# Weights decoded and split by a new plan, and earlier FFN units, in a thresholded attention with FFN

## The chip, the cores and the metric

The kernel runs on one core of a Trainium2 chip. The metric is device time in microseconds (us) from start to end of one execution. TensorE (PE) multiplies, VectorE (DVE), ScalarE (ACT) and GpSimd (POOL) work elementwise, SyncE (SP) issues the DMAs.

## What is computed

```python
def _attn_ref(q, k, v, tau):                 # 8 batches, 8 heads, 576 rows, 64 columns
    scores = scale * np.matmul(q, k.transpose(0, 1, 3, 2))
    thresh = np.max(scores, axis=-1, keepdims=True) - tau
    scores = np.where(scores >= thresh, scores, -1000000000.0)
    attn = np.exp(scores - np.max(scores, axis=-1, keepdims=True))
    attn = attn / (np.sum(attn, axis=-1, keepdims=True) + 1e-09)
    return np.matmul(attn, v)

def _moe_ref(x, w_in, w_out):                # 4608 tokens; w_in 512 x 2048, w_out 2048 x 512
    h = x @ w_in
    g = h * (1.0 / (1.0 + np.exp(-h)))
    return g @ w_out
```

The heads' results, put side by side, are the tokens x of the second function. The weights arrive as 64-bit floats, and the products are kept near fp32 by splitting operands into an upper and a lower f16 part.

## The kernel before

**Attention.** Work goes by tiles of 128 score rows of a head. A tile goes through: scores (L452 or L464, into one of two PSUM slots), row maximum (`soft1`, L474), exponential (L484, ScalarE), threshold and row sum (`soft2`, L493, VectorE, which frees the PSUM slot), normalising (`soft2b`), transposing (`soft3`), and, once a pair of heads is through, the product with v (`av`) and its split into x (`av_post`, L568 and L569). Batch 0 takes a "direct" form: its probabilities stay fp32, GpSimd normalises them (L507), TensorE transposes them (L403, L408) and ScalarE copies them out of PSUM (L416, L417). From batch 1 on ScalarE normalises (L511), GpSimd splits (L519 to L525) and DMAs transpose.

Batch 0 is worked in two halves: tiles 0 to 15 ("low") give x for its first 256 tokens, tiles 28 to 47 ("high") for the other 320. The indices 16 to 27 and 48 carry no tile; batch 1 begins at tile 49. The last index is about 300.

**Weights.** There are 16 chunks of w_in and 16 of w_out, 512 KB each. `load_weights` brings a chunk into a buffer: eight of w_in's into parts of `gbuf`, which later holds the FFN's inner values, the others in turn into two buffers of the pool `stage`. `decode_weights` turns 64-bit words into fp32: ScalarE L190, VectorE L193 and L196, then four matmuls (L208) whose diagonals give maxima. After 16 chunks `pow2_scales` makes a power-of-two scale of them (i_w for w_in, o_w for w_out). `split_weights` then makes the f16 parts in `wst`: for w_in GpSimd scales (L225), ScalarE rounds (L228), GpSimd subtracts (L229); for w_out ScalarE rounds with the scale (L220) and VectorE scales and subtracts in one instruction (L221).

**FFN.** A unit `h_unit` is 12 matmuls (L593) for 128 inner columns of one token range, with four elementwise steps behind it (L601 ScalarE, L602 VectorE, L608 ScalarE, L609 VectorE); a unit `o_unit` is 12 matmuls (L624), a quarter of the work for 128 output rows. For each of batch 0's two ranges there are 16 of each.

**What sets the order.** The main loop goes through the tile indices and writes, at each, the steps of a few tiles, the weights' steps that `W_PLAN` puts there, and as many FFN units as `credit` allows: it grows by `rate` per index, for batch 0 by `RATES`. A row of `W_PLAN` is first chunk, index of the first decode, index of the last, index at which the split ends, and a priority. A scheduler with a simulated timeline then orders each engine's instructions by these priorities and by what it holds to be ready; each engine runs its own list in that order. SP issues all loads in its list's order.

```python
W_PLAN = ((0, 0, 10, 13, 0), (16, 9, 22, 36, 0))
PRI_S, PRI_SOFT1, PRI_SOFT2 = 1600, 50, 200
```

## Time and profile before

| | |
|---|---|
| median of 3 runs | 1228.44 us (1227.75 to 1228.84) |
| the profiled execution: time | 1225.66 us |
| its span, first to last instruction | 1223.9 us |
| busy: PE, DVE, ACT, POOL | 1150.3, 933.7, 796.4, 707.5 us |
| mean granted TensorE clock, share of full | 0.987 |

Times of single instructions come from the profiled execution. The granted clock is the one of TensorE's two levels (1.2 and 2.4 GHz), as a share of the full one, averaged over a stretch. An engine's busy time in a stretch, set beside the stretch's length, tells whether it could have set the pace there; what ended the idle time ahead of an instruction tells whom it waited for.

### The profile page before, as it was taken

How to read it: one execution, taken by the hardware profiler on the slowest of the kernel's cores; microseconds unless marked ns; L12 is line 12 of the kernel's file. 1: busy time of each engine (PE TensorE's matmuls, PEld its weight loads, DVE VectorE, ACT ScalarE, POOL GpSimd, SP SyncE). 2: the span in 40 equal slices, each digit the busy share in tenths (PEclk: the TensorE clock that was granted, in tenths of full speed). 3: DMA queues.
4: the chain of work that ended last, by engine and by line, in shares of the span. 5: the costliest groups of instructions: out<-in, count | busy, mean ns of one | idle time of the engine just before them, and what ended most of it. 6: DMA issues, size and time to landing. Idle time of an engine off the chain costs nothing.

```text
span 1223.9 us, 27062 instructions
## 1 busy us (share of the span) xinstructions
PE 1150.3 (94%) x9474; PEld 899.2 (73%) x9474; DVE 933.7 (76%) x2625; ACT 796.4 (65%) x1505; POOL 707.5 (58%) x902
## 2 busy tenths in 40 slices
PE   6868799999899799999999999999999999999998
PEld 4545567777786577787777777788778877777777
DVE  7988988988999988889889858886788858333330
ACT  6667875876867777777777747785677756333331
POOL 2385357887877587886888428781778547100000
PEclk9979999999999999999999999999999999999999
DMA  9553148889788777886987448772877356200000
GB/s 309 185 161 95 41 108 173 160 160 177 132 177 141 160 137 139 150 165 151 167 149 145 114 94 155 146 136 82 153 150 142 77 92 116 42 11 16 16 10 25
DMA packets 340887, 151.73 MB, mean 124 GB/s; under 512 B 305936, under 2 KB 317200, under 8 KB 340752
## 3 DMA queue, kind: packets, MB, share of 16 engines
q1 hardware_dynamic: 340752, 150.01, 59.1%
q8 instruction: 75, 1.23, 0.4%
q14 instruction: 60, 0.49, 0.1%
HBM read 66.19 MB, written 9.44 MB: 62 GB/s over the span
## 4 chain that ended last, share of the span: by engine, by line
PE 63%; DVE 11%; DMA 10%; POOL 7%; issue 4%; ACT 4%; SPq 1%; POOLq 0%; ACTq 0%; DVEq 0%
PE o L624 24%; PE h L593 21%; PE s L464 9%; PE a L550 7%; DMA wT<-hl 4%; POOL hl L522 3%; DMA wraw<-in_w_out 3%; DVE w L493 2%; POOL hl L519 2%; DVE sm L474 2%; DVE qstack L350 2%; POOL hl L525 1%; DMA wraw<-in_w_in 1%; ACT w L484 1%; ACT w L511 1%
## 5 line engine op out<-in xcount | busy, mean ns | idle before, releaser
L593 PE MATMUL h<-x,wst 128*128 128x288 f16 (+2 forms) x3072 | 425.8, 288 | 7.8 <-DVE gbuf L609 5.0
L624 PE MATMUL o<-gbuf,wst 128*128 128x288 f16 (+2 forms) x3072 | 417.9, 286 | 2.4 <-ACT wst L634 2.4
L593 PEld LDWEIGHTS <-wst 128*128 128x128 f16 x3072 | 292.2, 98 | 95.7 <-issue 16.9
L624 PEld LDWEIGHTS <-wst 128*128 128x128 f16 x3072 | 292.7, 98 | 83.7 <-issue 7.4
L522 POOL TENSOR_TENSOR hl<-w,hl 128x512 f16<-128x512 f32 x252 | 302.6, 1201 | 12.8
L519 POOL TENSOR_SCALAR hl<-w 128x576 f16<-128x576 f32 x252 | 172.2, 686 | 193.4 <-ACT w L511 115.7
L484 ACT ACTIVATE w<-s,sm 128x576 f32<-128x576 f32 x288 | 211.6, 739 | 91.9 <-DVE sm L474 39.1
L493 DVE SCALAR_TENSOR_TENSOR w<-s,sm,w 128x576 f32<-128x576 f32 x288 | 232.0, 812 | 39.9 <-ACT w L484 37.8
L474 DVE TENSOR_REDUCE sm<-s 128x1 f32<-128x576 f32 x288 | 214.4, 749 | 28.7 <-PE s L464 21.8
L511 ACT ACTIVATE w<-w,sm 128x576 f32<-128x576 f32 x252 | 191.4, 771 | 52.1 <-DVE sm L501 50.1
L602 DVE SCALAR_TENSOR_TENSOR h<-th,h 128x288 f32<-128x288 f32 (+2 forms) x256 | 116.2, 455 | 113.7 <-ACT th L601 112.3
L601 ACT ACTIVATE th<-h,msc 128x288 f32<-128x288 f32 (+2 forms) x256 | 126.6, 498 | 103.2 <-PE h L593 101.8
L464 PE MATMUL s<-khi,qstack 128*128 128x288 f32 x560 | 144.3, 338 | 12.7 <-DVE w L493 9.9
L608 ACT ACTIVATE gbuf<-h 128x288 f16<-128x288 f32 (+2 forms) x256 | 104.3, 408 | 78.2 <-DVE h L602 77.5
L609 DVE SCALAR_TENSOR_TENSOR gbuf<-h,gbuf 128x288 f16<-128x288 f32 (+2 forms) x256 | 115.3, 452 | 41.9 <-ACT gbuf L608 41.0
L550 PE MATMUL a<-wT,v 128*64 128x288 f16 (+2 forms) x1568 | 115.0, 289 | 10.8 <-DMA wT<-hl 10.6
L360 POOL TENSOR_TENSOR klo<-kraw,khi 128x576 fp32r<-128x576 f32 x64 | 94.5, 1476 | 47.1 <-ACT khi L358 47.0
L464 PE MATMUL s<-klo,qstack 128*128 128x288 f32 x560 | 120.8, 296 | 0.0
L464 PEld LDWEIGHTS s<-khi,qstack 128*128 128x128 f32 x560 | 87.7, 190 | 31.9 <-issue 15.4
L550 PEld LDWEIGHTS <-v 128*64 128x64 f16 x1568 | 84.5, 110 | 33.7 <-issue 22.1
L464 PEld LDWEIGHTS s<-klo,qstack 128*128 128x128 f32 x560 | 90.4, 189 | 0.6
L525 POOL TENSOR_TENSOR hl<-w,hl 128x64 f16<-128x64 f32 x252 | 89.5, 355 | 0.0
(101 smaller groups left out, 930.4 us busy)
## 6 DMA issues: line engine op xcount, KB each, us to landing
kraw<-in_kT SPq DMA_DIRECT2D x128, 144.0 KB, 3.0
qraw<-in_qT SPq DMA_DIRECT2D x96, 144.0 KB, 3.0
vraw<-in_vL SPq DMA_DIRECT2D x32, 320.0 KB, 3.6
wraw<-in_w_out SPq DMA_DIRECT2D x16, 512.0 KB, 3.7
out_t<-wst SPq DMA_DIRECT2D x48, 144.0 KB, 2.1
wT<-hl SPq DMA_TRANSPOSE x280, 3.4
gbuf<-in_w_in SPq DMA_DIRECT2D x8, 512.0 KB, 6.2
wraw<-in_w_in SPq DMA_DIRECT2D x8, 512.0 KB, 5.1
```

The costliest lines, as they stand in the source:

```text
L464: nc.tensor.matmul(s_ps[:, j, :HALF], lhs, kk[:, j * HALF : (j + 1) * HALF], start=(n == 0), stop=(n == len(seq) - 1),)
L474: nc.vector.tensor_reduce(out=negm, in_=s_ps[:, :, :HALF], op=ALU.max, axis=AX.XY, negate=True)
L484: nc.scalar.activation(wtile[t].rearrange("p (j c) -> p j c", j=2), sps[t][:, :, :HALF], AF.Exp, bias=small[t][:, 0:1],)
L493: nc.vector.scalar_tensor_tensor(out=w3, in0=s_ps[:, :, :HALF], scalar=sm[:, 1:2], in1=w3, op0=ALU.is_ge, op1=ALU.mult, accum_out=sm[:, 2:3],)
L511: nc.scalar.activation(w, w, AF.Copy, scale=r)
L519: nc.gpsimd.tensor_scalar(out=fl[:, 0:S], in0=w, scalar1=1.0, scalar2=1.0, op0=ALU.mult, op1=ALU.mult)
L522: nc.gpsimd.tensor_tensor(out=fl[:, 640:1152], in0=w[:, 0:512], in1=fl[:, 0:512], op=ALU.subtract)
L550: nc.tensor.matmul(a_ps[odd * D : (odd + 1) * D, :n], vt[:, lo_v, odd, kv, :], wT[v, b * H + 2 * p + odd][:, kw, c0 - base : c0 - base + n ...
L593: nc.tensor.matmul(ph[:, :n], wi(c, f, lo_w), x16[b, lo_x][:, c, c0 : c0 + n], start=(k == 0), stop=(k == 11),)
L601: nc.scalar.activation(th[:, :n], ph[:, :n], AF.Tanh, scale=moe_sc[b][:, 0:1])
L602: nc.vector.scalar_tensor_tensor(out=ph[:, :n], in0=th[:, :n], scalar=1.0, in1=ph[:, :n], op0=ALU.add, op1=ALU.mult,)
L624: nc.tensor.matmul(ps[:, :n], wo(f, d, lo_w), g[:, lo_g, :n], start=(f == 0 and k == 0), stop=(f == NF - 1 and k == 2),)
```

## The change

- `RATES` goes from 0.9 units per index to 1.03 for the first range of batch 0 and to 1.45 for the second; and the first matmul of each of these units is held in program order against the others (`PACED`).
- The second row of `W_PLAN` gives w_out's loads, decodes and scale a priority of 150, and its split ends at index 38 instead of 36; the split itself has priority 0.
- Of the weights' chunks, those with i % 4 of 2 and 3 that had no place in `gbuf` get one (words 6400 and 7424), beside the two buffers of `stage`.
- The scale of w_out takes its column sum in the second half of the bank of the last weights' maximum instead of a bank of its own.
- `split_weights`: every second chunk of w_in goes the way that w_out went (ScalarE with the scale, L224, VectorE in one instruction, L225). The other eight stay with GpSimd (L230, L236). A chunk of w_out is now scaled by VectorE in fp32 (L234), rounded by ScalarE (L235), and subtracted by GpSimd (L236).
- `soft2b`: tiles 12 to 15 and 28 to 37 are normalised by ScalarE (L518) instead of GpSimd (L514, formerly L507).
- The direct tiles' transposes are written one index later, their product with v one later, and the FFN units that need it one later.

```diff
-RATES = (0.9, 0.9)
+PACED = 1
+RATES = (1.03, 1.45)
...
-W_PLAN = ((0, 0, 10, 13, 0), (16, 9, 22, 36, 0))
+W_PLAN = ((0, 0, 10, 13, 0), (16, 9, 22, 38, 150))
...
-        allp = bank([P, P], f"{name}_ps", own)
+        allp = wps[7][:, P : 2 * P] if name == "o_w" else bank([P, P], f"{name}_ps", own)
...
+        else:
+            o = (None, None, 6400, 7424)[i % 4]
+        if o is not None:
             t = gbuf.bitcast(I32)[:, o : o + 1024].rearrange("p (c w) -> p c w", w=2)
...
-        if i >= 4 * NK:
+        if i < 4 * NK and i % 2:
             nc.scalar.activation(hi, w, AF.Copy, scale=sc)
             nc.vector.scalar_tensor_tensor(
                 out=w16[:, i, 512:1024], in0=w, scalar=sc, in1=hi, op0=ALU.mult, op1=ALU.subtract
             )
             return
-        nc.gpsimd.tensor_scalar(
-            out=w, in0=w, scalar1=sc, scalar2=1.0, op0=ALU.mult, op1=ALU.mult
-        )
+        if i < 4 * NK:
+            nc.gpsimd.tensor_scalar(
+                out=w, in0=w, scalar1=sc, scalar2=1.0, op0=ALU.mult, op1=ALU.mult
+            )
+        else:
+            nc.vector.tensor_scalar(out=w, in0=w, scalar1=sc, scalar2=None, op0=ALU.mult)
         nc.scalar.activation(hi, w, AF.Copy)
         nc.gpsimd.tensor_tensor(
             out=w16[:, i, 512:1024], in0=w, in1=hi, op=ALU.subtract
...
-        if tiles[t][0] in direct:
+        if tiles[t][0] in direct and not 12 <= t < first_high + 10:
...
+                if b < PACED and k == 0:
+                    tc.keep_in_program_order(mm)
...
-            avs.setdefault(last_b + AV_LAG, []).append((v, p, c0, n))
+            avs.setdefault(last_b + AV_LAG + 1, []).append((v, p, c0, n))
             if p == NPAIR - 1:
-                ready.append((last_b + AV_LAG + 1, b, c0, n))
+                ready.append((last_b + AV_LAG + 2, b, c0, n))
...
-            at(t1 + i * (t2 - t1) // 16, pri(hp, lambda i=i + first: split_weights(i)))
+            at(t1 + i * (t2 - t1) // 16, pri(0, lambda i=i + first: split_weights(i)))
...
-        if live(t - 1):
+        if live(t - 1) and tiles[t - 1][0] not in direct:
             soft3(t - 1)
+        if live(t - 2) and tiles[t - 2][0] in direct:
+            soft3(t - 2)
```

How the engines' lists change is shown at three places. In the names, `w32_14` is the probability tile of tile 14, `sm` its row statistics, `wst` the weights, `s_33` the scores of tile 33, `th` and `h` an h unit's values (batch, first token, unit), `tm` and `tl` the transposed tile, `wT` its place in SBUF, and `o_0_0_1` the second 128 output rows of the first range.

GpSimd, from the normalising of the last low tiles on, before:

```order
L507 TENSOR_SCALAR w32_12_708<-w32_12_708,sm_12_707 128x576
L507 TENSOR_SCALAR w32_13_754<-w32_13_754,sm_13_753 128x576
L225 TENSOR_SCALAR wst_89<-wst_89,i_w_sc_612 128x512 x16
L229 TENSOR_TENSOR wst_89<-wst_89 128x512 x2
L507 TENSOR_SCALAR w32_14_795<-w32_14_795,sm_14_794 128x576
L507 TENSOR_SCALAR w32_15_839<-w32_15_839,sm_15_838 128x576
L507 TENSOR_SCALAR w32_28_1137<-w32_28_1137,sm_28_1136 128x576
L507 TENSOR_SCALAR w32_29_1154<-w32_29_1154,sm_29_1153 128x576
```

and after:

```order
L514 TENSOR_SCALAR w32_10_558<-w32_10_558,sm_10_557 128x576
L514 TENSOR_SCALAR w32_11_628<-w32_11_628,sm_11_627 128x576
L230 TENSOR_SCALAR wst_89<-wst_89,i_w_sc_597 128x512 x8
L236 TENSOR_TENSOR wst_89<-wst_89 128x512 x20
L514 TENSOR_SCALAR w32_38_1554<-w32_38_1554,sm_38_1553 128x576
L236 TENSOR_TENSOR wst_89<-wst_89 128x512 x4
L514 TENSOR_SCALAR w32_39_1591<-w32_39_1591,sm_39_1590 128x576
L514 TENSOR_SCALAR w32_40_1628<-w32_40_1628,sm_40_1627 128x576
```

The 16 scalings of w_in have become eight, the subtractions of w_in and w_out stand together in one piece of 20, and the normalisings of tiles 12 to 37 are gone from the list.

VectorE, around the threshold steps (L493, now L500) of tiles 32 and 33, before:

```order
L193 TENSOR_SCALAR wst_89<-wst_89 128x512
L213 TENSOR_REDUCE wmx_90<-wps_6_857 128x1
L196 SCALAR_TENSOR_TENSOR wst_89<-wraw_28_886,wst_89 128x512
L493 SCALAR_TENSOR_TENSOR w32_32_1287,sm_32_1286<-s_32_1244,sm_32_1286,w32_32_1287 128x576
L609 SCALAR_TENSOR_TENSOR gbuf_61<-h_0_0_0_944,gbuf_61 128x256
L497 TENSOR_SCALAR sm_32_1286<-sm_32_1286 128x1
L501 RECIPROCAL sm_32_1286<-sm_32_1286 128x1
L493 SCALAR_TENSOR_TENSOR w32_33_1328,sm_33_1327<-s_33_1290,sm_33_1327,w32_33_1328 128x576
L474 TENSOR_REDUCE sm_34_1372<-s_34_1331 128x1
```

and after:

```order
L576 SCALAR_TENSOR_TENSOR x16_0_1_472<-a_0_3_0_904,xscale_98,x16_0_0_471 128x256
L484 TENSOR_SCALAR sm_33_1322<-sm_33_1322,ntau_81 128x1
L309 SCALAR_TENSOR_TENSOR msc_0_762<-msc_0_762,o_w_sc_981 128x1
L234 TENSOR_SCALAR wst_89<-wst_89,o_w_sc_981 128x512 x14
L225 SCALAR_TENSOR_TENSOR wst_89<-wst_89,i_w_sc_597 128x512
L234 TENSOR_SCALAR wst_89<-wst_89,o_w_sc_981 128x512
L611 SCALAR_TENSOR_TENSOR h_0_0_0_924<-th_0_0_0_958,h_0_0_0_924 128x256
L611 SCALAR_TENSOR_TENSOR h_0_0_1_945<-th_0_0_1_1000,h_0_0_1_945 128x256
L234 TENSOR_SCALAR wst_89<-wst_89,o_w_sc_981 128x512
L500 SCALAR_TENSOR_TENSOR w32_32_1278,sm_32_1277<-s_32_1237,sm_32_1277,w32_32_1278 128x576
L500 SCALAR_TENSOR_TENSOR w32_33_1323,sm_33_1322<-s_33_1281,sm_33_1322,w32_33_1323 128x576
```

The last decodes no longer stand here; 16 scalings of w_out (L234) and a subtraction of w_in (L225) stand ahead of tile 32's threshold step. The 16 steps of w_out's split on VectorE before (L221) stood one or two at a time between the steps of tiles 39 to 47.

ScalarE, from the exponential of tile 44 on, before:

```order
L484 ACTIVATE w32_44_1772<-s_44_1742,sm_44_1771 128x576
L220 ACTIVATE wst_89<-wst_89,o_w_sc_1002 128x512
L416 ACTIVATE wT_6_5_1680<-tm_42_1747 128x4x128
L417 ACTIVATE wT_6_5_1680<-tl_41_1716 128x128
L484 ACTIVATE w32_45_1815<-s_45_1775,sm_45_1814 128x576
L220 ACTIVATE wst_89<-wst_89,o_w_sc_1002 128x512
L608 ACTIVATE gbuf_61<-h_0_0_8_1178 128x256
L601 ACTIVATE th_0_0_9_1278<-h_0_0_9_1219,msc_0_788 128x256
L416 ACTIVATE wT_7_6_1787<-tm_43_1780 128x4x128
L417 ACTIVATE wT_6_5_1680<-tl_42_1752 128x128
L608 ACTIVATE gbuf_61<-h_0_0_9_1219 128x256
L417 ACTIVATE wT_7_6_1787<-tl_43_1785 128x128
```

and after:

```order
L491 ACTIVATE w32_44_1782<-s_44_1752,sm_44_1781 128x576
L424 ACTIVATE wT_6_4_1643<-tl_40_1724 128x64
L424 ACTIVATE wT_6_5_1728<-tl_40_1724 128x64
L423 ACTIVATE wT_6_5_1728<-tm_41_1757 128x4x128
L617 ACTIVATE gbuf_61<-h_0_0_14_1393 128x256
L610 ACTIVATE th_0_0_15_1493<-h_0_0_15_1436,msc_0_762 128x256
L491 ACTIVATE w32_45_1827<-s_45_1785,sm_45_1826 128x576
L424 ACTIVATE wT_6_5_1728<-tl_41_1762 128x128
L423 ACTIVATE wT_6_5_1728<-tm_42_1790 128x4x128
L617 ACTIVATE gbuf_61<-h_0_0_15_1436 128x256
L645 ACTIVATE wst_89<-o_0_0_0_1480,msc_0_762 128x256
L645 ACTIVATE wst_89<-o_0_0_1_1646,msc_0_762 128x256
```

Where ScalarE was at the ninth and tenth h unit and still rounding w_out, it now does the last two h units and the first two outputs. Counted on TensorE's list: ahead of tile 40's scores stand 84 h matmuls instead of 36, ahead of tile 49's 192 h and 120 o matmuls instead of 144 and none.

## Rows read from the trace of the kernel before

**Rows 1.** Busy time, share of span and instructions of each engine (page)

```profile
PE 1150.3 (94%) x9474; PEld 899.2 (73%) x9474; DVE 933.7 (76%) x2625; ACT 796.4 (65%) x1505; POOL 707.5 (58%) x902
```

**Rows 2.** By stage: length; busy PE, PEld, DVE, ACT, POOL; PEclk, DMA share, GB/s

```profile
0.00:61.30 61.30, 46.10 (x285) 30.45 (x285) 51.54 (x166) 38.58 (x75) 16.59 (x30) 0.97 0.76 247
61.30:118.00 56.70, 42.42 (x233) 26.66 (x233) 46.90 (x117) 38.82 (x80) 43.23 (x44) 0.85 0.42 132
118.00:157.00 39.00, 31.56 (x213) 23.91 (x212) 34.87 (x92) 30.63 (x69) 9.98 (x9) 0.96 0.17 48
157.00:325.90 168.90, 157.04 (x1298) 122.86 (x1297) 148.59 (x421) 125.34 (x236) 132.68 (x164) 0.99 0.79 157
325.90:495.00 169.10, 156.96 (x1340) 122.97 (x1337) 153.61 (x429) 121.67 (x221) 125.90 (x163) 0.99 0.76 147
495.00:1223.90 728.90, 716.22 (x6116) 572.37 (x6115) 498.16 (x1404) 441.39 (x828) 379.16 (x494) 1.00 0.54 104
```

**Rows 3.** Timeline of TensorE: start, length, operation, idle before and releaser

```profile
61.28 1.24 PE L452 MATMUL s<-kd,gbuf 128*128 128x288 f32 x4 [0.85 <-DVE w L493]
...
118.05 1.24 PE L452 MATMUL s<-kd,gbuf 128*128 128x288 f32 x4
...
157.01 0.51 PE L464 MATMUL s<-khi,qstack 128*128 128x288 f32 x2
...
178.62 1.27 PE L624 MATMUL o<-gbuf,wst 128*128 128x256 f16 x10
```

**Rows 4.** Groups of ScalarE, 61.3 to 118 us: busy, mean ns, idle before

```profile
L190 ACT ACTIVATE wst<-wraw 128x512 f32<-128x512 f32 x14 | 9.4, 675 | 11.3 <-DMA wraw<-in_w_out 11.3
```

**Rows 5.** The chain that ended last, 52 to 113 us: start, length, what

```profile
52.62 3.47 DMA wraw<-in_w_out
...
56.59 4.51 DMA wraw<-in_w_out
...
112.50 1.31 PE h L593 x12
```

**Rows 6.** Timeline of GpSimd

```profile
60.02 12.72 POOL L225 TENSOR_SCALAR wst<-wst,i_w_sc 128x512 f32<-128x512 f32 x16 [2.51 <-DVE i_w_sc L145]
...
75.39 3.67 POOL L507 TENSOR_SCALAR w<-w,sm 128x576 f32<-128x576 f32 x4
```

**Rows 7.** Groups of VectorE, 0 to 61.3 us

```profile
L193 DVE TENSOR_SCALAR wst<-wst 128x512 int32<-128x512 int32 x18 | 7.9, 436 | 1.2 <-ACT wst L190 1.1
L196 DVE SCALAR_TENSOR_TENSOR wst<-wraw,wst 128x512 int32<-128x512 int32 x10 | 7.0, 698 | 0.0
```

**Rows 8.** Groups of VectorE, 61.3 to 118 us

```profile
L196 DVE SCALAR_TENSOR_TENSOR wst<-wraw,wst 128x512 int32<-128x512 int32 x14 | 13.2, 946 | 0.1
L193 DVE TENSOR_SCALAR wst<-wst 128x512 int32<-128x512 int32 x14 | 10.0, 712 | 6.3 <-ACT wst L190 6.3
...
L602 DVE SCALAR_TENSOR_TENSOR h<-th,h 128x256 f32<-128x256 f32 x3 | 1.2, 421 | 0.0
```

**Rows 9.** The weights' tile on VectorE, 0 to 160 us: duration ns min/median/max

```profile
L193 DVE TENSOR_SCALAR wst<-wst x32: 404/426/1281, 11.8 to 108.1; 128x512 int32<-128x512 int32 x32
L196 DVE SCALAR_TENSOR_TENSOR wst<-wraw,wst x24: 666/690/1527, 21.7 to 109.2; 128x512 int32<-128x512 int32 x24
L221 DVE SCALAR_TENSOR_TENSOR wst<-wst,o_w_sc x16: 726/743/1485, 124.6 to 150.3; 128x512 f16<-128x512 f32 x16
```

**Rows 10.** Groups of ScalarE, 0 to 200 us

```profile
L228 ACT ACTIVATE wst<-wst 128x512 f16<-128x512 f32 x16 | 10.0, 634 | 1.9 <-POOL wst L229 1.9
...
L601 ACT ACTIVATE th<-h,msc 128x256 f32<-128x256 f32 x16 | 7.3, 469 | 2.9 <-PE h L593 2.7
L511 ACT ACTIVATE w<-w,sm 128x576 f32<-128x576 f32 x9 | 6.8, 768 | 4.1 <-DVE sm L501 4.1
```

**Rows 11.** Groups of GpSimd, 61.3 to 118 us

```profile
L229 POOL TENSOR_TENSOR wst<-wst 128x512 f16<-128x512 f32 x16 | 21.4, 1355 | 3.6 <-ACT wst L228 3.6
...
L507 POOL TENSOR_SCALAR w<-w,sm 128x576 f32<-128x576 f32 x13 | 10.6, 822 | 8.2 <-DVE sm L501 3.3 <-DVE sm L497 2.7 <-PE tl L408 1.2
```

More of the change, by code (lines that the diff above doesn't have):

```diff
@@ L203, in decode_weights @@
         if c == 0:
-            wps[n] = bank([P, P], f"wps_{n}", 2)
+            wps[n] = bank([P, 2 * P if n == 7 else P], f"wps_{n}", 2)
         upper = w.bitcast(BF16).rearrange("p (c t) -> p c t", t=2)[:, :, 1]
@@ L208, in decode_weights @@
             nc.tensor.matmul(
-                wps[n], part, part,
+                wps[n][:, 0:P], part, part,
                 start=(c == 0 and j == 0), stop=(c == 3 and j == 3),
@@ L212, in decode_weights @@
         if c == 3:
-            nc.vector.tensor_reduce(out=wmx[:, n : n + 1], in_=wps[n], op=ALU.max, axis=AX.X)
+            nc.vector.tensor_reduce(out=wmx[:, n : n + 1], in_=wps[n][:, 0:P], op=ALU.max, axis=AX.X)
     def split_weights(i):
@@ L592, in h_unit @@
             for lo_w, lo_x in ((0, 0), (0, 1), (1, 0)):
-                nc.tensor.matmul(
+                mm = nc.tensor.matmul(
                     ph[:, :n], wi(c, f, lo_w), x16[b, lo_x][:, c, c0 : c0 + n],
@@ L623, in o_unit @@
             for k, (lo_w, lo_g) in enumerate(((0, 0), (0, 1), (1, 0))):
-                nc.tensor.matmul(
+                mm = nc.tensor.matmul(
                     ps[:, :n], wo(f, d, lo_w), g[:, lo_g, :n],
@@ L627, in o_unit @@
                 )
+                if b < PACED and f == 4 * quarter and k == 0:
+                    tc.keep_in_program_order(mm)
         def post():
```

## The prediction

> **What bounds the kernel now.** I read the busy shares first, then the stages, then the waits. TensorE is busy 94% of the span [rows 1], so only time that TensorE loses can be won. Where it loses it stands in the stage table [rows 2]. From 495 us on it is busy 716 of 728.9 us: little is to be had there. The first 157 us lose most: 46.10 busy of 61.3, 42.42 of 56.7, 31.56 of 39.0, thus 36.9 us idle, and part of the busy time ran at the lower of the two clock levels (mean granted clock 0.97, 0.85 and 0.96; of the busy time that is 3, 15 and 4%, or 1.4 + 6.4 + 1.3 us). The stages from 157 to 495 lose 24 us of 338.
>
> The borders of the stages are landmarks of the program on TensorE: the scores of tile 28 (first of the second half of batch 0) at 61.28, of tile 40 at 118.05, of tile 49 (first of batch 1) at 157.01; the first output unit of the FFN starts at 178.62 [rows 3]. The work in the two middle stages is not long; it is late. Three reasons can be read. ScalarE's decodes wait 11.3 us for the DMAs of w_out [rows 4]: with two buffers a load starts only after the decode of the one before last, and the chain of waits is made of such loads, 3.5 to 4.5 us each [rows 5]. GpSimd then scales 16 chunks of w_in in one go, 12.72 us from 60.02 on, with the normalising of tiles 14, 15, 28 and 29 queued behind it until 75.39 [rows 6]. And VectorE pays for sharing with GpSimd: a decode pair (L193, L196) costs 0.436 + 0.698 us in the first stage and 0.712 + 0.946 in the second, where GpSimd is busy 43.2 of 56.7 us [rows 2, 7, 8].
>
> **The change, part by part.** (1) Start to tile 28. The order now puts 28 decode pairs ahead of VectorE's step on tile 14, which frees the banks that tile 28 needs, instead of 18. This part costs: ten L193 at 0.436 and eight to nine L196 at 0.698 are 10 us [rows 7]; 2 us of that fit where VectorE is idle (51.54 busy of 61.3 [rows 2]). Tile 28 starts at 69 instead of 61.3. If VectorE's gaps took 4 us it would be 67; at the shared prices of [rows 8], 0.712 + 0.946, it would be 74, for there is a second cause for delay: the DMA engines are already 76% busy in this stage [rows 2] and the extra loads come on top.
>
> (2) Tile 28 to 40. VectorE is the longest here: 46.9 of 56.7 us [rows 2]. What goes: the decodes done earlier, ten L193 and eight L196 at the shared prices, 7.1 + 7.6 = 14.7 us [rows 8]. What comes: all 16 scalings of w_out in fp32 (L234), a form that the trace does not show. Its bounds are the single-input L193 of the same tile width, 404 ns at the least and 1281 at the most [rows 9]; I take 0.7, the mean of L193 beside a busy GpSimd [rows 8]: 11.2 us. Eight subtractions of w_in that leave GpSimd, at 743 ns, L221's median [rows 9]: 5.9 us. Four more h units with two steps of 0.42 each [rows 8]: 3.4 us. Sum 46.9 - 14.7 + 20.5 = 52.7 us. ScalarE, 38.8 us: ten decodes leave, 0.675 each [rows 4]; 12 normalisings at 0.768 (9.2), some 13 copies of w_out's upper parts at L228's 0.634 (8.2) and four h units with two steps of at most 0.47 (3.8) come [rows 10]: 53.2. GpSimd, 43.2 us: 13 normalisings, eight scalings and eight subtractions leave, 10.7 + 6.4 + 10.8; 16 subtractions at 1.355 come: 37 [rows 2, 6, 11], 20 subtractions stand in one piece. So VectorE and ScalarE fill the stage. Of VectorE's 9.8 us of idle time 6.3 were waits for a decode on ScalarE [rows 8], which itself waited for loads [rows 4]; with the loads ahead these go, and 52.7 + 3.5 = 56.2 us are left. With L234 at L193's median of 0.43 the stage takes 52, with 1.2 it takes 64. I take 57: tile 40 at 126 instead of 118. What hides the normalisings on ScalarE is the idle time that the loads leave; if the loads still come late, their 9.2 us fall on the chain to the transposes.
>
> (3) Tile 40 to 49. Here the faster rates of units tell. By the order, TensorE has 192 h matmuls and 120 o matmuls ahead of tile 49's scores, where it had 144 and none: 168 more, of which 48 lie ahead of tile 40. Twelve take 1.31 us [rows 5], so one takes 0.109 and the 120 of this stage 13.1 us; nine transposes fall behind, about 1 us less. TensorE's 31.56 us [rows 2] become 43.7, less the 1.3 that the low clock took: 42.4, and at 0.98 busy, as from 495 on, 43.3. VectorE's 34.87 [rows 2] lose the 16 L221, 11.9 us at their median [rows 9], and cannot hold this up. The stage is bound by TensorE: 43.5 us, between 41.5 and 46. Tile 49 starts at 169.5 instead of 157.0.
>
> (4) After tile 49. By then TensorE has done 168 x 0.109 = 18.3 us more FFN work, less 0.8 of transposes that stand behind: 17.5. So the end moves by 169.5 - 157.0 - 17.5 = -5.0 us if the rest takes what it took. By the order the lead stays at some 18 us of TensorE work to tile 140, is 11 at tile 150 and nothing by tile 216, so most of it is consumed after 495 us, where TensorE is 98% busy and less work is less time. I take the rest as neutral, by +-4.
>
> (5) At no cost: the maximum in half of a bank (same instructions), the four added buffer slots (no instruction), and the two delays of one tile for the transposes and the attention product. What hides these is that TensorE has h units to do meanwhile; without that cover, one tile of 4.3 us (39.0 / 9) once.
>
> The profiled execution took 1225.66 us, its span is 1223.9, and the median of the runs is 1228.44; the difference of 2.8 us lies between runs, so I move the median: 1228.4 - 5 = 1223.4, rounded to **1223**. By the bounds of the parts (67 to 74, 52 to 64, 41.5 to 46) the sum alone could run from -14 to +9.5 us.
>
> **Rivals.** *Dense fill, much faster.* If the earlier loads and the split work leave TensorE always with an h unit at hand, the whole piece from tile 28 to 49 runs as dense as from 495 on and at the full clock. TensorE's 42.42 x 0.85 + 31.56 + 17.5 = 85.1 us over 0.98 are 87 us, and with 69 to 73 ahead of it tile 49 comes at 156 to 160: gain 15 to 18, time 1210 to 1213. For it: h units can start once w_in is split, with or without scores. Against: VectorE and ScalarE each have 53 us of work between tiles 28 and 40 that TensorE's transposes wait for.
>
> *The scalings in a row, slower.* VectorE gets 14 scalings of w_out in one piece between the maximum of tile 33 and the masking of tile 32, and tile 34's scores wait for that masking. Beside it GpSimd has 20 subtractions in one piece. If each scaling takes what the slowest L193 took, 1.28 us [rows 9], the piece lasts 17.9 instead of 9.8 us at 0.7; with tile 28 at 73 tile 40 then comes at 138 and the time is 1223 + 12 = 1235. It decides from a mean of about 1.1 us on (14 x 0.4 = 5.6 us, all of the gain). For it: the stretched L221 and L196 at 1.49 and 1.53 [rows 9]. Against: the mean beside GpSimd was 0.712, not 1.28 [rows 8].
> The Trainium skill, page "SBUF — State Buffer", section "Who interferes with whom", states a stricter rule: such a VectorE instruction and a GpSimd one that reads SBUF exclude each other for a whole instruction, the later one fully blocked. By that rule each scaling would follow a whole subtraction, 0.43 + 1.36 = 1.79 us, 25 us for the 14, and the time would be near 1238. The trace agrees in part: the row's longest L193 is 0.85 us over its median, its mean only 0.28.
>
> *Given back, no change.* From 157 to 495 VectorE is busy 302.2 of 338 us, TensorE 314 [rows 2]. If VectorE sets the pace there, the 7 us of lead that are used up ahead of tile 150 buy nothing: 1228 to 1230. For it: 0.91 busy in the second of these stages. Against: TensorE is at 0.93 there, and only 3.4 us of VectorE's work move forward.
>
> **How the numbers follow.** A measurement tells about 0.2%, 2.5 us, from no change. Forecast (1218 to 1226) 0.38, dense fill 0.14, given back 0.20, scalings in a row 0.28. Faster is the first two, 0.52; same 0.20; slower 0.28. The range takes in the dense fill's better half and the scalings' price: 1211 to 1236. The likeliest case's own range is 1218 to 1226.
>
> **What would show it.** Right: tile 28's scores near 69 us; no wait of ScalarE for w_out's DMAs after that; no block of 12.7 us on GpSimd; L234 at a mean near 0.7; output units on TensorE before tile 47, by 160 us; tile 49 near 169 with TensorE over 0.95 busy from tile 40 on and no stretch at the lower clock there. Wrong: L234 over 1.1 us; tile 40 after 131; tile 49 after 175; or tile 49 as forecast and tile 150, which with 11 us of lead left should come at 501 (495 + 11 - 5), at 506: the third rival.

## The result, and the profile after

The changed kernel takes 1234.19 us, median of 14 runs (1229.84 to 1238.55), against 1228.42 for the kernel before; the ratio is 1.0050, 95% interval 1.0037 to 1.0063. It is slower by 5.8 us where 5 us less were forecast. The profiled execution took 1238.55 us, the slowest of the 14, while that of the kernel before (1225.66) was 2.8 us under its median: of the 12.9 us between the two spans some 7 belong to the two executions, not to the kernels.

The page's first part, to be read against [rows 1]:

```profile
PE 1154.7 (93%) x9474; PEld 902.4 (73%) x9474; DVE 930.3 (75%) x2633; ACT 805.8 (65%) x1519; POOL 700.3 (57%) x888
```

The table by stage, cut at the same tiles as [rows 2] (28, 40, 49, 100, 150), with the columns of that one:

```profile
0.00:72.47 72.47, 51.99 (x320) 35.56 (x320) 60.63 (x184) 46.82 (x89) 15.14 (x26) 0.93 0.88 281
72.47:130.75 58.28, 43.58 (x250) 29.65 (x248) 50.02 (x141) 50.17 (x103) 34.02 (x31) 0.85 0.12 38
130.75:173.84 43.09, 40.96 (x324) 33.51 (x322) 24.06 (x72) 22.27 (x56) 11.72 (x13) 1.00 0.17 49
173.84:354.28 180.44, 163.96 (x1385) 128.78 (x1383) 154.04 (x438) 131.33 (x245) 136.08 (x168) 1.00 0.75 155
354.28:516.94 162.66, 147.75 (x1177) 111.90 (x1178) 139.64 (x404) 116.72 (x208) 121.61 (x156) 0.97 0.75 145
516.94:1236.80 719.86, 706.46 (x6028) 562.96 (x6028) 501.87 (x1399) 438.51 (x823) 381.70 (x497) 1.00 0.53 105
```

TensorE's timeline at the landmarks of [rows 3]: scores of tiles 28 and 40, first output unit, scores of tile 49:

```profile
72.47 1.19 PE L459 MATMUL s<-kd,gbuf 128*128 128x288 f32 x4
...
130.75 1.14 PE L459 MATMUL s<-kd,gbuf 128*128 128x288 f32 x4
...
159.19 1.04 PE L633 MATMUL o<-gbuf,wst 128*128 128x256 f16 x8
...
173.84 0.51 PE L471 MATMUL s<-khi,qstack 128*128 128x288 f32 x2
```

The first three stages came as worked out: 72.5, 58.3 and 43.1 us against 69, 57 and 43.5. Up to tile 49 the kernel is 16.8 us later and has 17.9 us more of FFN matmuls behind it (counted on TensorE's list, 0.107 us for 256 columns): even, one microsecond ahead, instead of five. What made it slower came later. A number helps to see it, called the net delay here: the delay of a tile's scores against the kernel before, less the lead in FFN work at that tile. In the two profiles it is -1.0 us at tile 49, +1.0 at 57, +8.4 at 100, +12.8 at 160 and +12.9 at tile 299. u_lag, an experiment below whose units stand in the same places on TensorE's list ahead of tiles 49, 57 and 160, was profiled in an execution near its median; its net delay goes from -0.3 at tile 57 to +9.1 at 160 and is +7.6 at 299. So the loss lies between tiles 57 and 160 there too.

GpSimd's timeline, to be read against [rows 6]:

```profile
73.15 7.75 POOL L230 TENSOR_SCALAR wst<-wst,i_w_sc 128x512 f32<-128x512 f32 x8 [7.95 <-DVE sm L504]
...
100.42 1.40 POOL L236 TENSOR_TENSOR wst<-wst 128x512 f16<-128x512 f32 x1 [2.41 <-ACT wst L235]
102.83 1.47 POOL L236 TENSOR_TENSOR wst<-wst 128x512 f16<-128x512 f32 x1 [1.01 <-ACT wst L235]
107.39 1.15 POOL L236 TENSOR_TENSOR wst<-wst 128x512 f16<-128x512 f32 x1 [3.09 <-ACT wst L235]
```

VectorE's timeline, the scalings of w_out in a row:

```profile
97.95 7.43 DVE L234 TENSOR_SCALAR wst<-wst,o_w_sc 128x512 f32<-128x512 f32 x14
```

GpSimd's block has half the scalings and takes 7.75 us instead of 12.72. Its 20 subtractions are no piece at all: they come one to three at a time, with waits of 0.2 to 3.1 us for ScalarE's rounding between them. So only two of them slowed one of the 14 scalings, which took 0.53 us each. The scalings still hold up the scores: the threshold steps of tiles 32 and 33 stand behind them, and TensorE's next scores wait for these, at a granted clock of 0.66 from 100 to 115 us:

```profile
108.28 4.02 PE L459 MATMUL s<-kd,gbuf 128*128 128x288 f32 x8 [4.77 <-DVE w L500]
```

### The profile page after: what moved, and what is told of

It reads as the page before. It is cut to its first block, busy times and chain, and to the rows that moved or that the text cites. A ratio compares the mean times of both kernels' runs of the same rounds, so it can differ in the third digit from the quotient of the medians.

```text
span 1236.8 us, 27034 instructions
## 1 busy us (share of the span) xinstructions
PE 1154.7 (93%) x9474; PEld 902.4 (73%) x9474; DVE 930.3 (75%) x2633; ACT 805.8 (65%) x1519; POOL 700.3 (57%) x888
## 4 chain that ended last, share of the span: by engine, by line
PE 55%; DVE 14%; DMA 11%; ACT 7%; POOL 6%; issue 6%; SPq 1%; POOLq 0%; ACTq 0%; DVEq 0%
PE o L633 22%; PE h L600 18%; PE s L471 7%; PE a L557 6%; DMA wT<-hl 4%; DVE w L500 4%; DMA vraw<-in_vL 3%; DVE sm L481 3%; DVE qstack L357 2%; POOL hl L526 2%; POOL hl L529 2%; DVE h L611 1%; ACT w L491 1%; ACT w L518 1%; DMA gbuf<-in_w_in 1%
## 5 line engine op out<-in xcount | busy, mean ns | idle before, releaser
L600 PE MATMUL h<-x,wst 128*128 128x288 f16 (+2 forms) x3072 | 420.5, 286 | 11.5 <-DVE gbuf L618 9.3
L500 DVE SCALAR_TENSOR_TENSOR w<-s,sm,w 128x576 f32<-128x576 f32 x288 | 232.4, 813 | 42.9 <-ACT w L491 40.1
L518 ACT ACTIVATE w<-w,sm 128x576 f32<-128x576 f32 x266 | 200.6, 771 | 51.1 <-DVE sm L508 43.3
L471 PE MATMUL s<-khi,qstack 128*128 128x288 f32 x560 | 144.0, 338 | 14.0 <-DVE w L500 12.1
L471 PEld LDWEIGHTS s<-khi,qstack 128*128 128x128 f32 x560 | 87.4, 190 | 35.4 <-issue 16.9
L532 POOL TENSOR_TENSOR hl<-w,hl 128x64 f16<-128x64 f32 x252 | 94.8, 376 | 0.0
## 6 DMA issues: line engine op xcount, KB each, us to landing
kraw<-in_kT SPq DMA_DIRECT2D x128, 144.0 KB, 3.0
qraw<-in_qT SPq DMA_DIRECT2D x96, 144.0 KB, 2.9
out_t<-wst SPq DMA_DIRECT2D x48, 144.0 KB, 2.1
```

The source lines that it names most:

```text
L471: nc.tensor.matmul(s_ps[:, j, :HALF], lhs, kk[:, j * HALF : (j + 1) * HALF], start=(n == 0), stop=(n == len(seq) - 1),)
L500: nc.vector.scalar_tensor_tensor(out=w3, in0=s_ps[:, :, :HALF], scalar=sm[:, 1:2], in1=w3, op0=ALU.is_ge, op1=ALU.mult, accum_out=sm[:, 2:3],)
L518: nc.scalar.activation(w, w, AF.Copy, scale=r)
L600: mm = nc.tensor.matmul(ph[:, :n], wi(c, f, lo_w), x16[b, lo_x][:, c, c0 : c0 + n], start=(k == 0), stop=(k == 11),)
```

## The experiments

Medians are of 4 to 14 runs. Ratios are to runs of the kernel before on the same chip, with 95% intervals. "Lead" is FFN work ahead of the kernel before, in us on TensorE's list. Starts of tiles are those of their scores in each kernel's profile, one execution each: the changed kernel and aR100, which by the order differ only behind tile 90, are 5.2 us apart at tile 40, so a difference of that size between two profiles proves little by itself. The rows stand together here; each kernel's edit and what was expected follow.

| kernel | median us | ratio | tile 28 | 40 | 49 | 57 | 160 | lead at 57 | at 160 |
|---|---|---|---|---|---|---|---|---|---|
| before | 1228.4 | 1 | 61.3 | 118.1 | 157.0 | 189.1 | 525.9 | 0 | 0 |
| changed | 1234.2 | 1.0050 (1.0037 to 1.0063) | 72.5 | 130.8 | 173.8 | 207.0 | 549.0 | 16.9 | 10.4 |
| u_bufs | 1237.9 | 1.0082 (1.0060 to 1.0103) | 66.4 | 114.4 | 152.8 | 185.9 | 538.2 | -2.2 | 6.1 |
| u_split | 1234.6 | 1.0057 (1.0036 to 1.0077) | 73.5 | 125.4 | 156.8 | 190.7 | 531.9 | 12.2 | 4.0 |
| u_rates | 1238.6 | 1.0089 (1.0071 to 1.0107) | 72.4 | 131.5 | 171.3 | 210.0 | 545.8 | 16.9 | 9.7 |
| late | 1233.5 | 1.0044 (1.0028 to 1.0060) | 75.8 | 124.4 | 169.5 | 193.7 | 540.5 | 6.1 | 9.9 |
| u_lag | 1233.8 | 1.0043 (1.0026 to 1.0060) | 73.7 | 128.9 | 172.5 | 205.7 | 545.4 | 16.9 | 10.4 |
| u_norm | 1242.0 | 1.0103 (1.0084 to 1.0123) | 71.2 | 131.1 | 178.2 | 212.6 | 548.5 | 16.9 | 10.4 |
| o_rates | 1232.5 | 1.0027 (1.0009 to 1.0045) | 62.0 | 117.2 | 153.2 | 180.5 | 537.9 | 1.8 | 9.2 |
| o_bank | 1228.6 | 0.9998 (0.9981 to 1.0014) | 61.5 | 117.0 | 152.0 | 178.5 | 528.2 | -6.8 | -1.3 |
| o_lag | 1232.7 | 1.0026 (1.0005 to 1.0047) | 72.2 | 127.1 | 164.3 | 193.6 | 539.5 | 3.7 | -2.8 |
| o_norm | 1222.3 | 0.9946 (0.9926 to 0.9967) | 62.9 | 109.8 | 145.6 | 180.3 | 526.6 | -8.0 | 1.1 |
| o_bufs | 1233.4 | 1.0039 (1.0019 to 1.0058) | 73.0 | 129.6 | 161.0 | 191.4 | 532.6 | 8.3 | 4.4 |
| o_split | 1238.5 | 1.0077 (1.0057 to 1.0097) | 62.4 | 111.8 | 151.1 | 186.2 | 532.7 | -10.6 | -3.7 |
| n_14 | 1221.4 | 0.9946 (0.9928 to 0.9964) | 61.5 | 109.7 | 145.0 | 181.5 | 523.5 | -1.8 | 1.4 |
| n_all20 | 1236.0 | 1.0067 (1.0042 to 1.0092) | 61.5 | 110.6 | 144.0 | 177.9 | 526.3 | -9.3 | -8.8 |
| bD | 1216.4 | 0.9904 (0.9881 to 0.9926) | 62.6 | 120.1 | 159.6 | 192.0 | 523.3 | 0 | 2.8 |
| aD | 1227.7 | 1.0002 (0.9983 to 1.0020) | 71.2 | 134.5 | 177.6 | 212.6 | 553.9 | 16.9 | 19.1 |
| aR100 | 1229.2 | 1.0010 (0.9990 to 1.0031) | 72.4 | 136.0 | 179.0 | 214.1 | 551.6 | 16.9 | 16.6 |
| nR105 | 1213.8 | 0.9877 (0.9855 to 0.9898) | 62.5 | 113.7 | 149.1 | 185.0 | 527.0 | -1.8 | 6.8 |

**One part taken back, first four.** The theory at that point was "early pull": the added buffers let decodes stand ahead of tile 28, which makes it late. Its rivals were that the lead is given back behind tile 49, and that the new split is the cost.

u_bufs, the changed kernel with

```diff
-            o = (None, None, 6400, 7424)[i % 4]
+            o = None
```

> The changed kernel without the added buffer slots (w_out again through two buffers); all else as changed. In the order 76 column-sum matmuls of decoded chunks stand ahead of tile 28's scores instead of 108 (72 before the change), and the FFN lead at tile 49 falls from 17.9 us to -3.8. Theory 'early pull' (the decodes pulled ahead of tile 28 cost the 11 us by which tile 28 is later, and the lead only pays them back): tile 28 at 61 to 64 us, and a time near the kernel before, 1226 to 1231. Theory 'given back' (the lead is worth nothing behind tile 49, the loss lies there): also tile 28 near 62, but the stretch from tile 49 to 160, which lost 13 us against the work done in it, is as long as before the change: 1220 to 1226. Theory 'new split' (VectorE and GpSimd in each other's way): still slower than before, 1234 or more.

u_split, the changed kernel with the split of before (for w_in GpSimd scales and subtracts, for w_out VectorE does both in one):

```diff
-        if i < 4 * NK and i % 2:
+        if i >= 4 * NK:
             nc.scalar.activation(hi, w, AF.Copy, scale=sc)
```

> The changed kernel with the old split of the weights (GpSimd all of w_in, VectorE all of w_out in one instruction). Decodes as early as in the changed kernel (104 column-sum matmuls ahead of tile 15), but the lead at tile 49 is only 3.8 us. 'Early pull': tile 28 still near 72 us and less lead to pay for it: 1236 to 1242, slower than the changed kernel. 'New split': faster than the changed kernel, 1226 to 1230. 'Given back': the lead does not matter, so the same as the changed kernel within 2 us, 1232 to 1236.

u_rates:

```diff
-PACED = 1
-RATES = (1.03, 1.45)
+PACED = 0
+RATES = (0.9, 0.9)
```

> The changed kernel with the old rates (0.9 units per index) and no fixed program order of the units. The order keeps most of the lead: 14.7 us at tile 49 instead of 17.9, 16.9 at tile 57, and 0 instead of -4.6 at tile 216. 'Early pull' and 'new split': no difference from the changed kernel, 1232 to 1236. 'Given back' by way of the rates (units used up too early, so that TensorE lacks filling work later): 1227 to 1230.

late:

```diff
-W_PLAN = ((0, 0, 10, 13, 0), (16, 9, 22, 38, 150))
+W_PLAN = ((0, 0, 10, 13, 0), (16, 24, 32, 37, 150))
```

> The changed kernel with w_out's decodes planned at indices 24 to 32 instead of 9 to 22 and the end of the split at 37 instead of 38; four extra slots, shared split and rates as changed. The order has no w_out decode ahead of tile 28 (64 column-sum matmuls, 72 before the change), and a lead of 3.8 us at tile 49 and 6 at 57. 'Early pull': tile 28 near 58 to 60 us, earlier than before the change, tile 49 near 155 to 159, and a time below the kernel before, 1219 to 1226. 'Given back': the same 8 to 13 us are lost behind tile 49, 1230 or more. 'New split': slower than before, 1232 or more.

None came back to the kernel before, so taking back none of these parts alone mends it. u_bufs put tile 28 at 66.4 and tile 49 4 us earlier than before the change, and yet was slower than the changed kernel; of the theories only "new split" had allowed that, and u_split, the same as the changed kernel without the new split, speaks against it. u_split had tile 57 at 190.7 with a lead of 12 us, a gain of 10.6 us by the net delay above, and lost all of it by tile 65: it is the time that "given back" named. u_rates was slower than the changed kernel by 4 to 5 us, with nearly the same order; that has no explanation here. late did not do what its plan says: 30 of VectorE's L197 still started ahead of tile 28, as in the changed kernel (29), because the scheduler moved them up. It tells nothing of "early pull". My count of the column-sum matmuls on TensorE was the wrong measure for it.

**One part alone.** Each is the kernel before with one part; the lines are those of the change's diff, where no other is shown. o_rates has the `RATES` and `PACED` lines, o_bank the column sum in the last maximum's bank, o_lag the three later steps of direct tiles, o_norm this line:

```diff
-        if tiles[t][0] in direct:
+        if tiles[t][0] in direct and not 12 <= t < first_high + 10:
```

> The kernel before with the new rates and the fixed program order of batch 0's units, nothing else. No decode moves; in the order the FFN lead is 0 at tile 49, 8.0 us at tile 70, 11.1 at 100, 11.9 at 200 and 0 at 216. 'Given back' (between tiles 57 and 160 TensorE shares the pace with VectorE, so FFN work done earlier there shortens nothing): 1226 to 1231, no faster than before, and tile 160 later by about the lead, 8 to 10 us. 'Lead pays' (the forecast's step 4): tile 160 later by the lead as well, but from there the end 9 us earlier relative to it; a time of 1222 to 1228.

> The kernel before with the column sum of w_out's scale in the other half of the last maximum's bank, nothing else: the same instructions, in a changed order (the FFN lead is -3.8 us at tile 49, -8.1 at 80, 0 at 150). 'Order' (the order before suits the time from tile 57 to 160 well, and any shift of units there loses some of it, whatever the cause): 1231 to 1236, lost between tiles 57 and 160. All other theories, for which this edit is nothing: 1226 to 1230.

> The kernel before with the direct tiles' transposes written one index later, their product with v and the units behind it one later, nothing else. 'Lag' (the later transposes delay the first stages, which none of the kernels so far took back): tile 28 at 64 to 67 us, the time 1232 to 1238. 'Order': 1229 to 1234, with tile 28 within 2 us of 61.3. 'Given back': 1227 to 1230.

> The kernel before with tiles 12 to 15 and 28 to 37 normalised by ScalarE instead of GpSimd, nothing else. 'ScalarE is overloaded' (9 us of work more on ScalarE fall on the chain between tiles 12 and 40): tile 40 at 122 us or more instead of 118, time 1232 to 1237. 'Freed from the queue behind the 16 scalings' (GpSimd's block no longer holds tiles 14, 15, 28 and 29): tile 40 at 112 to 116, time 1224 to 1228. 'Order': tile 40 within 3 us, loss of 3 to 6 us between tiles 57 and 160.

o_rates is slower by 0.27%, 1232.5 us, a little above what either theory allowed: tile 57 came 8.6 us earlier, and then tiles 57 to 65 took 45.4 us instead of 26.9, with 6 us more of FFN work in them. o_bank is the same within 0.2%, so a shift of the order alone need not cost. o_lag: tile 28 at 72.2 us, later than any theory had it, with 20 decodes (L197) ahead of it where there had been 18. TensorE ran at its lower clock for much of the time from 27 to 48 us, around a product with v that waited for ScalarE's copies; in the kernel before the granted clock of the two stretches below was 0.89 and 1.00. Its table by stretches (columns as in [rows 2]):

```profile
20.00:35.00 15.00, 10.18 (x49) 5.67 (x46) 11.14 (x36) 10.40 (x20) 4.47 (x4) 0.74 0.89 283
35.00:48.00 13.00, 10.83 (x37) 6.84 (x37) 7.88 (x21) 6.29 (x12) 1.50 (x2) 0.64 0.37 113
```

Its timeline of TensorE:

```profile
28.37 4.71 PE L430 MATMUL a<-wT,vraw 128*64 128x256 f32 x16 [1.47 <-ACT wT L420]
33.02 2.29 PE L456 MATMUL s<-kd,gbuf 128*128 128x288 f32 x4
```

o_norm is the part that gains, 6.7 us. "Freed from the queue" was right in place, and the gain was larger than expected: tile 40 at 109.8. Its stage from tile 28 to 40:

```profile
62.91:109.75 46.84, 36.39 (x213) 22.92 (x214) 42.24 (x110) 42.24 (x86) 31.12 (x31) 0.96 0.48 156
```

Its groups of ScalarE there:

```profile
L515 ACT ACTIVATE w<-w,sm 128x576 f32<-128x576 f32 x12 | 9.4, 786 | 0.0
...
L194 ACT ACTIVATE wst<-wraw 128x512 f32<-128x512 f32 x13 | 9.0, 689 | 3.8 <-DMA wraw<-in_w_out 3.7
```

46.8 us instead of 56.8, at a granted clock of 0.96 instead of 0.85. ScalarE's wait for w_out's loads, 11.3 us in [rows 4], is 3.7 with the same two buffers: it had been the effect of a stage that stood still, not its cause.

Then the other two alone, and the other two taken back:

u_lag and u_norm are the changed kernel with the lines of o_lag and of o_norm taken back; o_bufs has the added slots alone (`o = (None, None, 6400, 7424)[i % 4]`: two places more, which with the two of `stage` make four for w_out; the prediction speaks of four added ones), o_split the new `split_weights` alone.

> The changed kernel with the direct tiles' transposes, products and units written where they were before; all else as changed. 'Lag' (the later transposes made tile 28 late, 72 us in the kernel that has this part alone): tile 28 at 63 to 67 us instead of 72.5 and the time 1228 to 1232. 'Early decodes' (28 decode pairs ahead of tile 28, as in the forecast): tile 28 at 68 to 73 and the time as changed, 1232 to 1236.

> The changed kernel with tiles 12 to 15 and 28 to 37 normalised by GpSimd as before; all else as changed. If the normalising on ScalarE, which alone gave -6.7 us, is worth the same here: tile 40 at 136 to 142 us instead of 130.8 and the time 1239 to 1243. If its gain was only to step around the block of 16 scalings, of which the new split leaves 8: tile 40 at 129 to 134, time 1233 to 1237.

> The kernel before with the four added raw slots in the buffer of the FFN's inner values, nothing else. In the order 112 column-sum matmuls stand ahead of tile 28 (72 before), the FFN lead is 3.8 us at tile 49 and 8.3 at 57. 'Early decodes': tile 28 at 67 to 72 us, and since the lead pays back part of it, tile 49 near 163 and 1230 to 1236. 'Loads were the bound' (ScalarE waited 11.3 us for w_out's loads between 61 and 118 us): tile 40 at or before 118, 1222 to 1227.

> The kernel before with the new shares of the split (8 chunks of w_in and w_out's scalings by VectorE, w_out's subtractions by GpSimd), nothing else. GpSimd's block has 8 scalings instead of 16. 'Block' (tiles 14, 15, 28, 29 queue behind GpSimd's scalings, and TensorE falls to its lower clock there): tile 40 at 110 to 115 us instead of 118, 1223 to 1227. 'VectorE's scalings hold up the scores': a gap of 6 to 8 us ahead of some tile's scores behind the scale of w_out, and an FFN lead that falls to -10.6 us at tile 57 and -19 at 80: 1231 to 1236.

o_bufs shows "early pull" by itself: tile 28 at 73.0, with 29 L197 ahead of it. The weights' tile on VectorE up to then (min/median/max, ns):

```profile
L197 DVE TENSOR_SCALAR wst<-wst x29: 404/416/627, 11.8 to 71.0; 128x512 int32<-128x512 int32 x29
```

The stage in its table:

```profile
0.00:73.00 73.00, 53.11 (x329) 35.78 (x329) 62.17 (x188) 47.33 (x90) 16.55 (x28) 0.93 0.85 284
```

u_lag kept tile 28 at 73.7 and did not change the time, as "early decodes" said, so in the changed kernel the lag costs nothing that can be measured; two causes can each make tile 28 late, and they do not add up. u_norm lost 0.5% against the changed kernel: the normalising on ScalarE is worth as much there as alone. It gains in another place, though: without it tile 40 comes at 131.1, hardly later, and tile 49 at 178.2 instead of 173.8. o_split has tile 40 6 us earlier, as "block" says, and then loses, more than expected: from tile 40 to 49 TensorE runs at 0.75 of its clock with a lead that falls to -10.6 us at tile 57 and -19 at 80. The stage:

```profile
111.81:151.06 39.25, 28.11 (x153) 19.96 (x153) 34.95 (x95) 22.60 (x49) 22.97 (x22) 0.75 0.14 39
```

Here the scalings in a row cost 0.84 us each, and no scores start between 126.24 and 143.31 us. VectorE's timeline:

```profile
125.18 10.07 DVE L234 TENSOR_SCALAR wst<-wst,o_w_sc 128x512 f32<-128x512 f32 x12
```

The single parts sum to +13.5 us (o_rates 3.5, o_bank -0.4, o_lag 3.6, o_norm -6.7, o_bufs 4.2, o_split 9.3), the whole is +5.8: the parts do not add up. u_bufs, which has everything but the new slots and is 10.2 us slower than the kernel before, shows the other parts together to cost more without the slots. The plan's new priority and the later end of the split were not tried alone.

**What takes the lead back, and what the gain hangs on.** bD and aD are the kernels before and changed with VectorE's last step of the h units of batches 1 to 7 left out:

```diff
+            if b == 0:
-            nc.vector.scalar_tensor_tensor(
+                nc.vector.scalar_tensor_tensor(
...
-                    ps[:, :n], wo(f, d, lo_w), g[:, lo_g, :n],
+                    ps[:, :n], wo(f, d, lo_w), g[:, lo_g if b == 0 else 0, :n],
```

> The kernel before without VectorE's last step of each h unit of batches 1 to 7 (the lower part of the FFN's inner value, L609, 0.45 us); the o units read the upper part twice instead, so that TensorE has the same number of matmuls. This is the base for the next kernel. If VectorE sets the pace between tiles 57 and 160: this stretch shrinks from 336.8 us to about TensorE's busy time there, 312 to 325, and the whole to 1200 to 1216. If it does not: the stretch stays above 332 and the whole above 1222.

> The changed kernel with the same step left out in the same way. In the order all stands as in the changed kernel up to tile 100. 'VectorE took the lead back': with VectorE relieved the FFN work done early is worth its time, tiles 57 to 160 lose at most 3 us against the base with the same step left out, and the time is that base -4 to +2 us. 'Lost whatever VectorE does' (the order of TensorE's units against the scores and the transposing DMAs): 8 to 13 us are lost there as in the changed kernel, and the time is the base + 4 to 9.

n_all20 and n_14 are the kernel before with, in the line of o_norm, `not 12 <= t < first_high + 20` and `not 14 <= t < first_high + 6`.

> The kernel before with tiles 12 to 15 and 28 to 47 normalised by ScalarE (the one part that gained, carried on to the last direct tile), nothing else. If GpSimd's normalising between its subtractions holds up the transposes in tiles 38 to 47 too: tile 49 at 140 to 144 us (145.6 with the part as it is) and 1219 to 1223. If only the block of 16 scalings mattered: no further gain, 1221 to 1226, since ScalarE then has eight normalisings more beside w_out's rounding.

> The kernel before with tiles 14, 15 and 28 to 33 alone normalised by ScalarE: those which GpSimd normalised behind or right after its block of 16 scalings. 'Block': the stretch at the lower clock from 73 to 87 us is gone, tile 40 at 108 to 112 us, and the time 1221 to 1225, as with all 14 tiles. If the gain comes from GpSimd's load as a whole: less than half of it, 1225 to 1229.

bD fell between its two expectations, 331.3 us for the stretch and 1216.4 for the whole. With VectorE relieved the changed kernel is 11.3 us slower than its base, more than the 5.8 before, so "VectorE took the lead back" is not borne out; but one step was taken off VectorE, which is still busy 281 of 331 us in bD, not all of its work. The pair shows one thing more: by tile 160 aD still has 16.3 us of lead over bD, nearly the 16.9 of tile 57, and yet its stretch is 10.0 us longer with the same FFN work (198.6 against 199.2 us). So time is lost there that no lead used up accounts for, though up to 7 us of it may belong to the two executions, which lie that much further apart than the medians.

n_14, eight tiles, gains the whole 6.7 us: the block of 16 scalings is still there, but no normalising queues behind it. GpSimd's timeline in n_14:

```profile
60.25 12.71 POOL L229 TENSOR_SCALAR wst<-wst,i_w_sc 128x512 f32<-128x512 f32 x16 [2.62 <-DVE i_w_sc L146]
72.93 2.71 POOL L233 TENSOR_TENSOR wst<-wst 128x512 f16<-128x512 f32 x2
```

The stretch from 73 to 87 us, in the kernel before and in n_14 (columns as in [rows 2]):

```profile
73.00:87.00 14.00, 8.80 (x39) 5.61 (x40) 10.43 (x24) 7.43 (x14) 10.57 (x10) 0.52 0.53 164
73.00:87.00 14.00, 10.93 (x73) 7.00 (x69) 12.84 (x33) 12.91 (x26) 8.91 (x7) 1.00 0.56 185
```

The granted clock there goes from 0.52 to 1.00, as "block" said. A rival, that VectorE's decodes become cheaper beside a less busy GpSimd, is too small: from tile 28 to 40 L197 (L193 before) takes 0.650 us in the mean instead of 0.712, and L200 (L196) 0.950 instead of 0.946, some 0.9 us in all where tile 40 comes 8.4 us earlier.

n_all20 brought tile 49 to 144.0 us, 13 earlier than before, as expected, and yet was slower by 0.67%, 1236.0 us where 1219 to 1226 were expected: behind it the lead falls to -17.7 us at tile 80, and tiles 100 to 120 then take 80.8 us instead of 68.8. So neither a gain nor a loss at tile 49 is the result.

The last two hold the lead beyond tile 160, `RATE = 0.95` changed to 1.0 in the changed kernel (aR100) and to 1.05 in n_14 (nR105).

> The changed kernel with the rate factor of all later units at 1.0 instead of 0.95, nothing else. The order is the same up to tile 90; then the lead is not used up ahead of tile 160: 16.7 us at tile 160 and 24.6 at 200 instead of 10.4 and 13.3, nothing at 240. 'Lead is lost where it is used ahead of tile 160 and paid behind it' (tiles 57 to 160 take about 339 us with 190 or with 196 us of FFN work in them): the same 336 to 345 us from 57 to 160 with 6 us more of FFN work, and 1226 to 1230. 'Early FFN work only displaces other work': 57 to 160 takes 6 us longer, 1231 to 1237.

> The kernel before with tiles 14, 15 and 28 to 33 normalised by ScalarE (1221.4 us) and the rate factor of later units at 1.05 instead of 0.95. In the order the lead is 9.2 us at tile 150 instead of 1.8, 7.1 at 200 and 0 at 216. 'Paid behind 160': tile 160 at 523 to 527 us (523.5 without), 1214 to 1219. 'Displaces': tile 160 at 529 to 532, 1220 to 1225.

The stretch from tile 57 to 160 (columns as in [rows 2]), in the kernel before:

```profile
189.10:525.90 336.80, 314.66 (x2662) 247.94 (x2661) 301.23 (x849) 249.31 (x455) 265.55 (x340) 0.99 0.80 156
```

In the changed kernel:

```profile
207.00:549.00 342.00, 314.25 (x2609) 244.62 (x2607) 294.36 (x853) 249.76 (x451) 267.45 (x340) 0.99 0.76 151
```

In bD:

```profile
192.00:523.30 331.30, 316.72 (x2695) 249.74 (x2694) 280.99 (x801) 249.64 (x457) 268.89 (x341) 1.00 0.79 159
```

In aD:

```profile
212.60:553.90 341.30, 320.90 (x2680) 252.18 (x2678) 285.62 (x804) 253.38 (x461) 267.29 (x339) 0.98 0.78 155
```

In aR100:

```profile
214.10:551.60 337.50, 314.74 (x2659) 247.70 (x2657) 296.76 (x855) 251.33 (x458) 268.65 (x341) 1.00 0.78 154
```

In nR105:

```profile
185.00:527.00 342.00, 326.85 (x2767) 258.16 (x2765) 292.34 (x851) 252.98 (x458) 265.00 (x341) 1.00 0.78 152
```

The FFN work in it is 196.4 us before; with the lead at 160 less that at 57 added it is 189.9 in the changed kernel, u_lag and u_norm (342.0, 339.7 and 335.9 us long) and 196.2 in aR100 (337.5): 6.3 us more of work, in no more time. In n_14 and nR105 it is 199.7 and 205.1, in 342.0 us both. All 18 kernels with the whole computation tell it less sharply: the nine with 188 to 196.4 us of FFN work took 335.8 to 345.9 us, 339.6 in the mean, without any trend among them; the nine with 197 to 205.5 took 342.0 to 357.4, 348.0 in the mean. So below some 196 us FFN work taken out of this stretch does not shorten it, and the changed kernel, with 189.9, lost the lead that it used up there; above that the pair n_14 and nR105 had the added work for nothing, while the seven others took 346.3 us and more. The stretch also tends to be shorter where tile 57 starts later, and no run separates that start from the work. Behind tile 160 a lead is paid: from there to tile 299 the changed kernel takes 497.5 us and the kernel before 508.3, with 10.9 us less FFN work in the changed one, 10.8 us for 10.9. aR100 is 5.0 us faster than the changed kernel (the profiled run of aR100, 1236.6 us, was the slowest of its 12, and lost 5 us more than the changed kernel's ahead of tile 40). nR105 is 7.6 us faster than n_14 by the medians, 8.5 by the ratios: 1213.8, 1.2% below the kernel before, the fastest kernel with the whole computation in this study. The rate acts on all later units, and the kernel before with a higher rate alone was not run: how much of these two gains is the lead kept and how much the rate's own is open (behind tile 160 nR105 took 9.5 us less than n_14 with 5.5 us less FFN work left). What sets the floor of some 336 us is not settled. VectorE has a part in bD (331.3 us, with 2.8 us more of FFN work) and none in aD (341.3).

## Why the prediction was wrong

Faster by 5 us was forecast with 0.52 for faster at all; the kernel is slower by 5.8, inside the range and on the other side. The time lies near the 1235 of the rival "scalings in a row", but not by its sum: that is chance.

- **Step 1, start to tile 28: right in cause, 3.5 us short.** 72.5 us, inside 67 to 74. Eleven more L193 than in [rows 7] stand ahead of tile 28, and VectorE was busy 9.1 us more, as counted. But its idle time did not absorb 2 us; it grew from 9.8 to 11.8, and the granted clock fell from 0.97 to 0.93. o_bufs shows the same start, 73.0, from the slots alone. Step 5 had the two delays of one tile at no cost: alone they put tile 28 at 72.2 us and cost 3.6 us (o_lag), at a time when no h units were there to cover them; in the changed kernel taking them back gained nothing that can be measured (u_lag).
- **Step 2, tile 28 to 40: right, 58.3 against 57.** VectorE 50.0 against 52.7 busy, ScalarE 50.2 against 53.2. The parts of it were mixed: a scaling cost 0.53 instead of 0.7; and the normalising that I put at nothing for the chain is the one part of the change that gains (o_norm -6.7 us alone; u_norm, without it, +6.5 against the changed kernel by the ratios). I had read GpSimd's block [rows 6] and costed only the work moved, not the queue behind it, and so did not see that eight normalisings alone would lift the stretch at the lower clock.
- **Step 3, tile 40 to 49: right, 43.1 against 43.5.** TensorE 40.96 of 43.09 us busy at the full clock, output units from 159.2 us, 15 us ahead of tile 49.
- **Step 4, "the rest as neutral": this step failed.** I knew from the order that 7 us of the lead are used up ahead of tile 150 and named it as a rival, "given back", at 0.20, but took its price out of the sum because TensorE was 93% busy there. The runs show that the 6.5 us of lead used up between tiles 57 and 160 bought nothing: the three kernels with this order took 339 us in the mean against 337 although they had 6.5 us less to do. The sign named for it came, and stronger: tile 150 at 516.9 us, 11 us behind the 506 of that rival, 4.3 of them from tile 49. The sum is then -5, +3.5 and +1.3 from steps 1 and 2, -0.4 from 3, +6.5 for the lead: +5.9, where +5.8 were measured. That it fits so closely is in part luck: the terms come from single executions, and the stretch's own 2.4 us more would make it +8. The cause that I gave that rival, VectorE's pace, is not borne out by bD and aD; why the stretch does not become shorter stays open, and by aD part of the loss may have another cause than the lead.
- **The rivals.** "Scalings in a row": its place was right, and the scores did wait there, 4.77 us idle on TensorE; but the longer scalings that it priced did not come, 7.43 us for 14 where 9.8 were in the sum and 17.9 in the rival. They came in o_split. What decided was not how many subtractions stand in GpSimd's list but whether ScalarE's rounding, which they wait for, lets them run at the same time. "Dense fill" did not come: the stage from 28 to 40 stayed at a clock of 0.85.

## What to carry to other kernels

Work done early pays only where it would else have been on the path; follow the lead to the place where it is used up, and price it there: in a stretch whose length does not follow its work it was worth nothing here, in one where the engine is 98% busy nearly all of it. When an engine's long block stands in front of a few short instructions that another engine waits for, and its clock falls meanwhile, move the few (here eight normalisings for 6.7 us), not the block and not everything of their kind. An order made by a scheduler follows neither the plan's indices nor one engine's list: count the instructions on the engine that pays.
